# Seven half-size output products in place of eight, in sixteen chunks of a fused attention and feed-forward kernel

## The chip, the cores and the metric

One core of one Trainium2 chip. The metric is device time of the whole program in microseconds (us), lower is better. All times that are compared here are of runs in the fast state (the two probe runs are single executions of unknown state, and only their traces are used); a run's time is the median of its executions, and each ratio is against executions of the kernel before on the same chip. The experiments ran on several chips, where the kernel before took 569.3 to 569.8 us, and differences to the changed kernel go across them. Where I give a ratio it is the mean time of the fast runs of one kernel over that of the other's fast runs of the same rounds, so not quite the ratio of the medians that I quote. Profiles are single executions; their span is some 2 us shorter than the time.

## The reference

```python
# q, k, v: (4, 5824, 256) float32; w1, w2: 256x1024; w3: 1024x1024; w_out: 1024x256
qn = q / (norm(q, axis=1) + 1e-6);  kn = k / (norm(k, axis=1) + 1e-6)
a  = softmax(kn.transpose(0, 2, 1) @ qn / tau)     # one 256x256 matrix per batch
x  = (v @ a).reshape(23296, 256)
h  = ((x @ w1) * (x @ w2)) @ w3
out = h @ w_out                                     # (23296, 256) float32
```

## The kernel before

The kernel folds the softmax matrix into w1 and w2 (one pair `Wf` per batch) and w3 into w_out (one 1024x256 matrix `W_sb`). So each batch is out = ((v Wf1) * (v Wf2)) W. It works through a batch in 12 chunks: eleven of 512 tokens and a last one of 192. A chunk has 8 slots, one for each 128 of the 1024 features. In a slot TensorE makes a and b, ScalarE casts a to bf16 in SBUF, VectorE multiplies it with b (still in PSUM), and two slots later TensorE multiplies the product ab with its rows of W, four matmuls of 256 columns:

```python
def emit_ab(b, c, j):
    for w in range(2):                                   # a, then b
        t = psum.tile([P, 512], F32, tag="ab", ..., bufs=4)
        ...                                              # two matmuls of 512 columns
    a_sb = work.tile([P, 512], BF16, tag="a_sb", ..., bufs=4)
    nc.scalar.copy(a_sb[:, :n], tiles[0][:, :n])
    ...
        nc.vector.tensor_mul(ab, a_sb, tiles[1])
    pend.append((b, c, j, ab))

def emit_out(b, c, j, ab, only=None):
    lhs = [ab[:, i * P : (i + 1) * P] for i in range(4)]
    ...
        nc.tensor.matmul(tl[h][:, o, :], lhsT=lhsT, rhs=W_sb[:, j, :], ...)
    ...                                                  # after slot 7:
        nc.scalar.copy(o[:, 0:2, :], tl[0])
        nc.vector.tensor_copy(o[:, 2:4, :], tl[1])
```

While batch b runs, the scores and the softmax of batch b + 1 are made in between. A planner places them: it keeps a clock of TensorE's work, and each piece has a time at which it is put into the engines' queues. `t1` is when the scores end, 98 in the middle batches, which is in chunk 8. The softmax is this list (its second column is the time after `t1 + 1`):

```python
def norms():
    nc.vector.tensor_add(a1, accs[n][:, 0], accs[n][:, 1])
    nc.gpsimd.partition_all_reduce(tot, a1, P, ReduceOp.add)
...
    [(0.0, 0.0, norms), (0.0, 5.5, k_row)]
    + [(0.0, 5.5 + 1.2 * i, lambda i=i: k_step(i)) for i in range(4)]
    + [(0.0, 6.0, q_sums), (0.0, 8.5, lambda: q_norm(st["ss"]))]
    + [(0.0, 10.3 + 1.2 * ct, lambda ct=ct: scale(ct)) for ct in range(CT)]      # VectorE
    + [(0.0, 11.0 + 1.2 * ct, lambda ct=ct: exps(ct)) for ct in range(CT)]       # ScalarE
    + [(0.2, 14.6, sums)]                                                        # TensorE
    + [(0.43, 15.6 + 1.1 * i, lambda i=i: fold(i)) for i in range(8)]            # TensorE, then ACT or DVE
```

Of the kernel before, what the change touches and what calls it, by code (L numbers as in the profile page):

```python
# [12 lines left out]
F32 = DT.float32  # L13
BF16 = DT.bfloat16

P = 128
PIECE = 8
LAG = 2
LAG_END = 5
IN_BUFS = {"q": 5, "k": 6, "v": 3}  # L20
MM_COL = 1.0 / 2400.0
MM_FIX = 0.0025

# [2 lines left out]
def kernel(  # L26
# [73 lines left out]
    pieces = {}  # L100

    def new_piece(nm, n, pi):
        t = in_pool.tile([P, PIECE, C], BF16, tag=nm, name=f"{nm}_{n}_{pi}", bufs=IN_BUFS[nm])
        pieces[nm, n, pi] = t
        if pi == NP_ - 1:
            if nm != "v":
                nc.vector.memset(t[LEFT:, LAST, :], 0.0)
            nc.gpsimd.dma_start(out=t[:LEFT, LAST, :], in_=qk_main[nm, n][1])
# [332 lines left out]
    def at(t, cost, fn):  # L441
        seq[0] += 1
        agenda.append((t, seq[0], cost, fn))
# [12 lines left out]
        return vTt[:, ct, :]  # L456

    last_ab = [None]
    held = [None]

    def gate():

# [7 lines left out]
    def emit_ab(b, c, j):  # L470
        n = chunk_cols(c)
        tiles = []
        for w in range(2):
            t = psum.tile([P, 512], F32, tag="ab", name=f"{'ab'[w]}_{b}_{c}_{j}", bufs=4)
            for ct in range(CT):
                nc.tensor.matmul(  # L476
                    t[:, :n], lhsT=Wf[b][:, ct, w, j * P : (j + 1) * P], rhs=rhs_of(b, c, ct),
                    start=(ct == 0), stop=(ct == CT - 1),
                )
            tiles.append(t)  # L480
        a_sb = work.tile([P, 512], BF16, tag="a_sb", name=f"as_{b}_{c}_{j}", bufs=4)
        nc.scalar.copy(a_sb[:, :n], tiles[0][:, :n])  # L482
        if c == NCH - 1:
            if b % 2 == 0 and j == 0:
                lefts[b // 2] = work.tile([P, FT, 2, P + LEFT], BF16, tag="left", name=f"left_{b}", bufs=1)
            both = lefts[b // 2][:, j, b % 2, :]
            nc.vector.tensor_mul(both, a_sb[:, :n], tiles[1][:, :n])  # L487
            ab = both[:, :P] if b % 2 == 0 else both[:, LEFT:]
        else:
            if b == 0 and c < 2:  # L490

                if j % 4 == 0:
                    held[0] = in_pool.tile([P, 4, 512], BF16, tag="q", name=f"abq_{c}_{j}", bufs=IN_BUFS["q"])
                ab = held[0][:, j % 4, :]
            else:
                ab = work.tile([P, 512], BF16, tag="ab_sb", name=f"abs_{b}_{c}_{j}", bufs=8 * NDEF + 2)
            nc.vector.tensor_mul(ab, a_sb, tiles[1])  # L497
        pend.append((b, c, j, ab))
        last_ab[0] = ab
        clock[0] += 4 * (n * MM_COL + MM_FIX)  # L500

    def emit_out(b, c, j, ab, only=None):
# [42 lines left out]
            if only is None:  # L545
                del out_tiles[b, c]

    NDEF = 4

    def load_qk(n, pi):  # L550
        load_piece("q", n, pi)
        load_piece("k", n, pi)
# [17 lines left out]
    def transpose_w3():  # L570

        for h in range(FT // 2):
            m = in_pool.tile([P, 2, FT, P], BF16, tag="k", name=f"w3T_{h}", bufs=IN_BUFS["k"])
            nc.sync.dma_start_transpose(m, w3_bf[:, 2 * h : 2 * h + 2, :])
            w3T.append(m)

# [89 lines left out]
    def make_agenda(b):  # L666
        agenda.clear()
        clock[0] = 0.0
        n = b + 1
        if b == 0:  # L670
            at(0.5, 0.87, soft0[5])
            for i in range(4):
                at((1.7, 2.6, 3.5, 3.9)[i], 0.43, soft0[7 + i])
            at(0.0, 0.0, load_library)
            at(4.6, 0.5, lambda: transpose_half_on_pe(0, 0, 1, False))
            at(7.0, 0.5, lambda: transpose_half_on_pe(0, 1, 0, True))
            at(8.0, 0.5, lambda: transpose_half_on_pe(0, 1, 1, False))
            at(15.0, 0.0, transpose_w3)
            at(15.0, 0.0, lambda: transpose_piece(0, 2))
            for jt in range(FT):  # L680
                at(27.5 + 1.2 * jt, 0.87, lambda jt=jt: w_unit(jt))
            moves = [("qk", 1, 0, 29.0), ("v", 0, 3, 30.0), ("v", 0, 4, 30.5), ("qk", 1, 1, 44.0), ("qk", 1, 2, 45.0)]
            moves += [("qk", 1, 3, 53.0), ("qk", 1, 4, 55.0), ("v", 0, 5, 61.0), ("qk", 1, 5, 73.0)]
            moves += [("v", 1, 0, 88.0), ("v", 1, 1, 98.0), ("v", 1, 2, 120.0), ("qk", 2, 0, 130.0)]
            t0, t1 = 54.0, 113.0
        else:
            moves = [("v", b, 3, 1.0), ("qk", n, 1, 10.0), ("qk", n, 2, 17.0), ("v", b, 4, 26.0), ("qk", n, 3, 38.0)]
            moves += [("v", b, 5, 46.0), ("qk", n, 4, 58.0), ("qk", n, 5, 66.0)]
            moves += [("v", n, 0, 76.0), ("v", n, 1, 86.0), ("v", n, 2, 96.0), ("qk", n + 1, 0, 108.0)]
            moves = [m for m in moves if m[1] < B]  # L690
            t0, t1 = 16.0, 98.0

        before = (0, 2) if b == 0 else None
        for nm, m, pi, t in moves:
            if before is not None and not (nm == "v" and before == (m, pi - 1) == (0, 3)):
                at(t, 0.0, lambda w=before: hold(vTs[w[0]][1][:1, 0, :1] if w[1] == NP_ - 1 else vTs[w[0]][0][:1, w[1] * PIECE, 0, :1]))
            at(t, 0.0, gate)
            if nm == "qk":
                at(t, 0.0, lambda m=m, pi=pi: load_qk(m, pi))
                before = None  # L700
            else:
                at(t, 0.0, lambda m=m, pi=pi: load_piece("v", m, pi))
                at(t + 4.0, 0.0, lambda m=m, pi=pi: transpose_piece(m, pi))
                before = (m, pi)
        if n == B:
            agenda.sort()
            return
        units = score_units(n)
        for i, (cst, fn) in enumerate(units):
            at(t0 + (t1 - t0) * i / len(units), cst, fn)  # L710
        soft = soft_units(n)
        for cst, t, fn in soft:
            at(t1 + 1.0 + t, cst, fn)
        agenda.sort()

    for b in range(B):
        make_agenda(b)
        for c in range(NCH):
            for j in range(FT):
                run_due()  # L720
                emit_ab(b, c, j)
                npop = 0
                lag = LAG
                if b == B - 1 and c >= NCH - 2:
                    lag = LAG_END if c == NCH - 1 else LAG + (LAG_END - LAG) * (j + 1) // FT
                while w_ready[0] and len(pend) > lag and npop < 2:
                    emit_out(*pend.pop(0))
                    npop += 1
                    run_due()
        run_due(1e9)  # L730

    n = len(pend)
    for i, only in [(i, 1) for i in range(n - 1)] + [(i, 0) for i in range(n - 2)] + [(n - 1, 1), (n - 2, 0), (n - 1, 0)]:
        emit_out(*pend[i], only=only)


# [33 lines left out]
```

## Time and profile before

| | kernel before |
|---|---|
| time, median of 4 runs | 569.77 us (569.47 to 570.15) |
| span of the profile | 567.7 us |
| a slot of the last batch | 1.30 us, all of it TensorE |
| a chunk of the last batch | 10.40 us |
| start of chunk 8 to start of the next batch, second batch | 40.40 us |
| the same, third batch | 39.57 us |

All chunk times below are differences between the starts of the first a matmul of two chunks in the trace. The page and the timeline are read in the prediction.

### The profile page before, as it was taken

To read this page: it belongs to the slowest core of one execution; us is meant where nothing else is said; L and a number is where in the kernel's file an instruction comes from. 1 tells how busy PE (TensorE), PEld (TensorE's weight loads), DVE (VectorE), ACT (ScalarE), POOL (GpSimd) and SP (SyncE) were. 2 spreads that over 40 slices of the span, in tenths; PEclk is the share of its full clock that TensorE was granted. 3 is DMA by queue.
4 is the path that set the end of the run, shared out by engine and by line. 5 is a ranking of instruction groups with operands and counts; after the bars stand their busy time and mean duration, and the time that the engine had idled before them with its cause. 6 is when DMAs were issued, how large, how long until landed. Compare 5 with 4: busy or idle time off the path is not lost.

```text
span 567.7 us, 10095 instructions
## 1 busy us (share of the span) xinstructions
PE 557.6 (98%) x3755; PEld 355.4 (63%) x3755; DVE 375.4 (66%) x581; ACT 338.7 (60%) x627; POOL 77.9 (14%) x163
## 2 busy tenths in 40 slices
PE   8799999999999999999999999999999999999997
PEld 5664566776656666666656566666655655665655
DVE  1047645888966577888766668787876665565564
ACT  1057536777766577777675567777765554454453
POOL 4260013120111111121210101030120000000000
PEclk9999999999999999999999999999999999999999
DMA  9999989978455796595661595765740325221011
GB/s 213 211 182 209 173 171 237 226 164 192 115 142 121 143 192 148 90 193 123 145 149 75 97 219 117 155 120 121 185 112 39 85 74 149 64 68 71 38 70 61
DMA packets 75104, 77.45 MB, mean 136 GB/s; under 512 B 54192, under 2 KB 58800, under 8 KB 75056
## 3 DMA queue, kind: packets, MB, share of 16 engines
q0 software_dynamic: 15760, 38.93, 39.3%
q1 hardware_dynamic: 59008, 37.23, 22.0%
q10 hardware_dynamic: 288, 0.66, 0.4%
q8 instruction: 29, 0.48, 0.3%
q14 instruction: 19, 0.16, 0.1%
HBM read 78.91 MB, written 23.86 MB: 181 GB/s over the span
## 4 chain that ended last, share of the span: by engine, by line
PE 93%; DMA 5%; ACT 1%; POOL 0%; issue 0%; DVE 0%; ACTq 0%; POOLq 0%
PE o L521 28%; PE b L476 28%; PE a L476 28%; PE G L192 5%; DMA k<-in_k_dram 5%; PE fold L363 2%; PE w L649 1%; ACT kr L283 0%; PE quarter L389 0%; POOL k L111 0%; POOL q L111 0%; PE sqk L225 0%; PE row L271 0%; ACT e L322 0%; ACT Wf L398 0%
## 5 line engine op out<-in xcount | busy, mean ns | idle before, releaser
L497 DVE TENSOR_TENSOR abs<-as,b 128x512 bf16<-128x512 bf16 x336 | 230.6, 687 | 143.9 <-ACT as L482 131.4
L482 ACT CAST as<-a 128x512 bf16<-128x512 f32 (+1 forms) x384 | 215.9, 562 | 170.4 <-DVE abs L497 84.7
L476 PEld LDWEIGHTS <-Wf 128*128 128x128 bf16 x1536 | 149.0, 98 | 102.3 <-ACT Wf L398 0.6
L476 PE MATMUL a<-vT,Wf 128*128 128x512 bf16 x704 | 209.6, 379 | 0.4 <-ACT Wf L398 0.4
L476 PE MATMUL b<-vT,Wf 128*128 128x512 bf16 x704 | 209.6, 379 | 0.0
L521 PE MATMUL o<-W_sb,abs 128*128 128x256 bf16 x1344 | 201.5, 273 | 0.0
L521 PEld LDWEIGHTS <-abs 128*128 128x128 bf16 x1344 | 131.2, 98 | 79.8 <-issue 0.2
L201 DVE TENSOR_TENSOR acc<-acc,sq 128x1024 f32<-128x1024 f32 x66 | 80.4, 1219 | 0.6 <-ACT sq L189 0.6
L192 PE MATMUL G<-k,q 128*128 128x256 bf16 x276 | 49.8, 273 | 0.0
L189 ACT ACTIVATE sq<-q 128x512 f32<-128x512 bf16 x66 | 41.8, 633 | 0.0
L189 ACT ACTIVATE sq<-k 128x512 f32<-128x512 bf16 x66 | 41.5, 629 | 0.0
L464 POOL COPY gate_t<-abs 1x1 bf16<-1x1 bf16 x39 | 10.5, 269 | 171.7 <-DVE abs L497 168.8
L543 DVE COPY osb<-o 128x512 f32<-128x512 f32 x44 | 30.1, 685 | 0.9 <-PE o L521 0.9
L192 PEld LDWEIGHTS <-q 128*128 128x128 bf16 x276 | 27.0, 98 | 3.1
L542 ACT COPY osb<-o 128x512 f32<-128x512 f32 x44 | 25.8, 586 | 4.1 <-PE o L521 2.1
L468 POOL COPY gate_t<-vT 1x1 bf16<-1x1 bf16 x16 | 3.1, 193 | 158.8 <-DMA vT<-v 158.8
L111 POOL DMA_DIRECT2D q<-in_q_dram x28 | 15.1, 540 | 12.5 <-DMA k<-in_k_dram 5.5
L370 ACT ACTIVATE Wf<-fold,rs 128x512 bf16<-128x512 f32 x15 | 10.3, 687 | 10.9 <-PE fold L363 8.7
L283 ACT ACTIVATE kr<-row 128x256 f32<-128x256 f32 x1 | 0.4, 383 | 26.1 <-PE row L271 26.1
L363 PE MATMUL fold<-w,e 128*128 128x512 bf16 x56 | 15.0, 379 | 0.0
L487 DVE TENSOR_TENSOR left<-as,b 128x192 bf16<-128x192 bf16 x32 | 11.3, 354 | 5.1 <-ACT as L482 2.7
L497 DVE TENSOR_TENSOR abq<-as,b 128x512 bf16<-128x512 bf16 x16 | 10.8, 686 | 5.0 <-ACT as L482 4.5
(98 smaller groups left out, 242.3 us busy)
## 6 DMA issues: line engine op xcount, KB each, us to landing
out_dram<-osb SPq DMA_DIRECT2D x44, 512.0 KB, 3.3
k<-in_k_dram POOLq DMA_DIRECT2D x19, 512.0 KB, 8.3
v<-in_v_dram POOLq DMA_DIRECT2D x19, 512.0 KB, 5.2
q<-in_q_dram POOLq DMA_DIRECT2D x18, 512.0 KB, 5.8
w_wout<-in_moe_w_dram POOLq DMA_DIRECT2D x1, 2048.0 KB, 22.7
k<-in_k_dram POOLq DMA_DIRECT2D x4, 320.0 KB, 8.8
v<-in_v_dram POOLq DMA_DIRECT2D x4, 320.0 KB, 4.9
q<-in_q_dram POOLq DMA_DIRECT2D x3, 320.0 KB, 4.1
```

Source lines behind the costliest of these rows:

```text
L111: nc.gpsimd.dma_start(out=pieces[nm, n, pi][:, lo:hi, :], in_=qk_main[nm, n][0][:, pi * PIECE + lo : pi * PIECE + hi, :])
L189: nc.scalar.activation(out=dst[:, :, part, :], in_=src[:, o : o + 2, :], func=AF.Square)
L192: nc.tensor.matmul(G[:, ct, :], lhsT=qt[:, i, ct * P : (ct + 1) * P], rhs=kt[:, i, :], start=(pr == 0 and part == 0 and ct == 0), stop=(pr ...
L201: nc.vector.tensor_add(accs[n], accs[n], sqs[0])
L363: nc.tensor.matmul(m, lhsT=st["e"][:, c2, c1 * P : (c1 + 1) * P], rhs=w12[:, c2, w, lo:hi], start=(c2 == 0), stop=(c2 == CT - 1),)
L476: nc.tensor.matmul(t[:, :n], lhsT=Wf[b][:, ct, w, j * P : (j + 1) * P], rhs=rhs_of(b, c, ct), start=(ct == 0), stop=(ct == CT - 1),)
L482: nc.scalar.copy(a_sb[:, :n], tiles[0][:, :n])
L487: nc.vector.tensor_mul(both, a_sb[:, :n], tiles[1][:, :n])
L497: nc.vector.tensor_mul(ab, a_sb, tiles[1])
L521: nc.tensor.matmul(tl[h][:, o, :], lhsT=lhsT, rhs=W_sb[:, j, :], start=(j == 0 and o == 0), stop=(j == FT - 1 and (small or o == 1)), skip ...
L542: nc.scalar.copy(o[:, 0:2, :], tl[0])
L543: nc.vector.tensor_copy(o[:, 2:4, :], tl[1])
```

## The change

A chunk's output is a product of 512x1024 by 1024x256. Cut in halves along all three sizes, it is eight products of half-size blocks; Strassen's and Winograd's scheme does it with seven, at the price of sums of blocks. So 32 matmuls of 256 columns become 56 of 128 columns, seven eighths of the columns. The change does this in 16 of the 44 large chunks: ten of the last batch, and chunks 0, 8 and 9 of the second and third batch. A chunk of this kind stays open until all its slots are done; its seven products then stand in the first seven slots of the next chunk. VectorE makes four sums (128x1024, bf16, all operands in SBUF) and three joins (PSUM added to the output), ScalarE four keeps (PSUM copied to the output); one copy on each goes. The ab tiles must live longer, so q, k, v, ab and the rest share one ring of 22 buffers.

```diff
-IN_BUFS = {"q": 5, "k": 6, "v": 3}
+BIG_BUFS = 22
+    def seven(b, c):
+        return c < NCH - 2 if b == B - 1 else b > 0 and c in (0, NCH - 4, NCH - 3)
...
+        def sum1():
+            nc.vector.tensor_add(s1, a21, a22)
+        def p1():
+            st["o"] = work.tile([P, 4, D], F32, tag="o_sb", ...)
+            nc.vector.tensor_sub(s2, s1, a11)
+            product("A", a11, w1, True)          # 8 matmuls of 128 columns
+            keep(0, 0)
+        def p5():
+            nc.vector.tensor_sub(s3, a11, a21)
+            product("C", s1, t1, True)
+        def p6():
+            product("A", s2, t2)                 # adds to A
+            keep(0, 1)
+        def p7():
+            nc.vector.tensor_sub(s4, a12, s2)
+            product("A", s3, t3)
+            keep(1, 1)
+        def p2():
+            product("B", a12, w21, True)
+            join("B", 0, 0)
+        def p4():
+            join("C", 1, 1)
+            product("A", a22, t4)
+            keep(1, 0)
+        def p3():
+            product("C", s4, w22)                # adds to C
+            join("C", 0, 1)
...
+        if not seven(b, c):
+            pend.append((slot[0] + LAG, 1, lambda only=None: emit_out(b, c, j, ab, only)))
+        elif j == FT - 1:
+            fns = seven_products(b, c, *halves)
+            fns[0]()
+            pend.extend((slot[0] + 1, 2, fn) for fn in fns[1:])
```

(Cut: the four combined weight blocks, made once in the first batch, and the bookkeeping of the queue of pending work.)

More of the change, by code (lines that the diff above doesn't have):

```diff
@@ L102, in new_piece @@
     def new_piece(nm, n, pi):
-        t = in_pool.tile([P, PIECE, C], BF16, tag=nm, name=f"{nm}_{n}_{pi}", bufs=IN_BUFS[nm])
+        t = in_pool.tile([P, PIECE, C], BF16, tag="big", name=f"{nm}_{n}_{pi}", bufs=BIG_BUFS)
         pieces[nm, n, pi] = t
@@ L458, with combine_weights @@
     last_ab = [None]
-    held = [None]
+    halves = [None, None]
+    slot = [0]
+    comb = {}
+    def seven(b, c):
+        return c < NCH - 2 if b == B - 1 else b > 0 and c in (0, NCH - 4, NCH - 3)
+    def combine_weights(step):
+        b11, b12 = W_sb[:, 0:4, :P], W_sb[:, 0:4, P:]
+        b21, b22 = W_sb[:, 4:8, :P], W_sb[:, 4:8, P:]
+        if step == 0:
+            comb["T"] = in_pool.tile([P, 4, 4, P], BF16, tag="big", name="comb_T", bufs=BIG_BUFS)
+            for nm in ("S12", "S34"):
+                comb[nm] = in_pool.tile([P, 2, 4, 2 * P], BF16, tag="big", name=f"comb_{nm}", bufs=BIG_BUFS)
+            comb["f"] = in_pool.tile([P, 2, 4, P], F32, tag="big", name="comb_f", bufs=BIG_BUFS)
+        T, f = comb["T"], comb["f"]
+        if step == 0:
+            nc.vector.tensor_sub(f[:, 0], b12, b11)
+        elif step == 1:
+            nc.scalar.copy(T[:, 0], f[:, 0])
+            nc.vector.tensor_sub(f[:, 1], b22, f[:, 0])
+        elif step == 2:
+            nc.scalar.copy(T[:, 1], f[:, 1])
+            nc.vector.tensor_sub(T[:, 2], b22, b12)
+        else:
+            nc.vector.tensor_sub(T[:, 3], b21, f[:, 1])
@@ new lines, in seven_products, with product, quarter, keep @@
+    def seven_products(b, c, k1, k2):
+        T = comb["T"]
+        a11, a21 = k1[:, :, : 2 * P], k1[:, :, 2 * P :]
+        a12, a22 = k2[:, :, : 2 * P], k2[:, :, 2 * P :]
+        s1, s2 = comb["S12"][:, 0], comb["S12"][:, 1]
+        s3, s4 = comb["S34"][:, 0], comb["S34"][:, 1]
+        w1 = [W_sb[:, j, :P] for j in range(4)]
+        w21 = [W_sb[:, 4 + j, :P] for j in range(4)]
+        w22 = [W_sb[:, 4 + j, P:] for j in range(4)]
+        t1, t2, t3, t4 = ([T[:, i, j, :] for j in range(4)] for i in range(4))
+        st = {}
+        def product(nm, a, w, first=False):
+            if first:
+                st[nm] = psum.tile([P, 2, P], F32, tag="out", name=f"prod{nm}_{b}_{c}", bufs=3)
+            for j in range(4):
+                for i in range(2):
+                    nc.tensor.matmul(
+                        st[nm][:, i, :], lhsT=a[:, j, i * P : (i + 1) * P], rhs=w[j],
+                        start=(first and j == 0 and i == 0), stop=(j == 3), skip_group_check=True,
+                    )
+            clock[0] += 8 * (P * MM_COL + MM_FIX)
+        def quarter(r, d):
+            return st["o"][:, 2 * r : 2 * r + 2, d * P : (d + 1) * P]
+        def keep(r, d):
+            nc.scalar.copy(quarter(r, d), st["A"])
+        def join(nm, r, d):
+            nc.vector.tensor_add(quarter(r, d), st[nm], quarter(r, d))
+        def sum1():
+            nc.vector.tensor_add(s1, a21, a22)
+        def p1():
+            st["o"] = work.tile([P, 4, D], F32, tag="o_sb", name=f"osb_{b}_{c}", bufs=3)
+            nc.vector.tensor_sub(s2, s1, a11)
[21 more added lines that the diff above has]
+            join("C", 0, 1)
+            rows = out[b * N : b * N + NT * P, :].rearrange("(p i) c -> p i c", i=NT)
+            nc.sync.dma_start(out=rows[:, 4 * c : 4 * c + 4, :], in_=st["o"])
+        return [sum1, p1, p5, p6, p7, p2, p4, p3]
@@ L489, in emit_ab @@
         else:
-            if b == 0 and c < 2:
-                if j % 4 == 0:
-                    held[0] = in_pool.tile([P, 4, 512], BF16, tag="q", name=f"abq_{c}_{j}", bufs=IN_BUFS["q"])
-                ab = held[0][:, j % 4, :]
-            else:
-                ab = work.tile([P, 512], BF16, tag="ab_sb", name=f"abs_{b}_{c}_{j}", bufs=8 * NDEF + 2)
+            if j % 4 == 0:
+                halves[j // 4] = in_pool.tile([P, 4, 512], BF16, tag="big", name=f"abh_{b}_{c}_{j}", bufs=BIG_BUFS)
+            ab = halves[j // 4][:, j % 4, :]
             nc.vector.tensor_mul(ab, a_sb, tiles[1])
-        pend.append((b, c, j, ab))
         last_ab[0] = ab
+        slot[0] += 1
+        if not seven(b, c):
[4 more added lines that the diff above has]
+            pend.extend((slot[0] + 1, 2, fn) for fn in fns[1:])
         clock[0] += 4 * (n * MM_COL + MM_FIX)
@@ L546, in emit_out @@
                 del out_tiles[b, c]
-    NDEF = 4
     def load_qk(n, pi):
@@ L572, in transpose_w3 @@
         for h in range(FT // 2):
-            m = in_pool.tile([P, 2, FT, P], BF16, tag="k", name=f"w3T_{h}", bufs=IN_BUFS["k"])
+            m = in_pool.tile([P, 2, FT, P], BF16, tag="big", name=f"w3T_{h}", bufs=BIG_BUFS)
             nc.sync.dma_start_transpose(m, w3_bf[:, 2 * h : 2 * h + 2, :])
@@ L704, in make_agenda @@
                 before = (m, pi)
+        if b == 0:
+            for i in range(4):
+                at(115.0 + 3.0 * i, 0.0, lambda i=i: combine_weights(i))
         if n == B:
@@ L721 @@
                 emit_ab(b, c, j)
-                npop = 0
-                lag = LAG
+                lag = 0
                 if b == B - 1 and c >= NCH - 2:
                     lag = LAG_END if c == NCH - 1 else LAG + (LAG_END - LAG) * (j + 1) // FT
-                while w_ready[0] and len(pend) > lag and npop < 2:
-                    emit_out(*pend.pop(0))
-                    npop += 1
+                room = 2
+                while w_ready[0] and len(pend) > lag and pend[0][0] <= slot[0] and pend[0][1] <= room:
+                    _, size, fn = pend.pop(0)
+                    fn()
+                    room -= size
                     run_due()
@@ L733 @@
     for i, only in [(i, 1) for i in range(n - 1)] + [(i, 0) for i in range(n - 2)] + [(n - 1, 1), (n - 2, 0), (n - 1, 0)]:
-        emit_out(*pend[i], only=only)
+        pend[i][2](only=only)
 _INS = ['q', 'k', 'v', 'tau', 'moe_w1', 'moe_w2', 'moe_w3', 'moe_w_out']
```

## The prediction

> **What bounds the kernel now.** I read the page first, for the busy shares and the chain that ended last; then the timeline of the steady stretch of the last batch, for what sets a period; then the timeline of the first stage, where narrow matmuls already run; then the groups, for durations.
>
> ```profile
> span 567.7 us, 10095 instructions
> PE 557.6 (98%) x3755; PEld 355.4 (63%) x3755; DVE 375.4 (66%) x581; ACT 338.7 (60%) x627; POOL 77.9 (14%) x163
> PEclk9999999999999999999999999999999999999999
> PE 93%; DMA 5%; ACT 1%; POOL 0%; issue 0%; DVE 0%; ACTq 0%; POOLq 0%
> ```
>
> The chain of work that ended last is 93% TensorE; the 5% DMA is the first 30 us, which the change doesn't touch. Busy TensorE alone proves little, so look at starts:
>
> ```profile
> 504.76 0.59 PE L476 MATMUL a<-vT,Wf 128*128 128x512 bf16 x2
> 505.19 0.59 PE L476 MATMUL b<-vT,Wf 128*128 128x512 bf16 x2
> 505.39 0.59 ACT L482 CAST as<-a 128x512 bf16<-128x512 f32 x1 [0.71 <-DVE abs L497]
> 505.63 0.60 PE L521 MATMUL o<-W_sb,abs 128*128 128x256 bf16 x4
> 506.01 0.69 DVE L497 TENSOR_TENSOR abs<-as,b 128x512 bf16<-128x512 bf16 x1 [0.61 <-ACT as L482]
> 506.06 0.60 PE L476 MATMUL a<-vT,Wf 128*128 128x512 bf16 x2
> ...
> 508.61 0.69 DVE L497 TENSOR_TENSOR abs<-as,b 128x512 bf16<-128x512 bf16 x1 [0.61 <-PE o L521]
> 508.65 0.58 ACT L542 COPY osb<-o 128x512 f32<-128x512 f32 x1
> 508.66 0.59 PE L476 MATMUL a<-vT,Wf 128*128 128x512 bf16 x2
> 509.22 0.68 DVE L543 COPY osb<-o 128x512 f32<-128x512 f32 x1
> ```
>
> A slot (one of 8 feature blocks of a chunk of 512 tokens) takes 506.06 - 504.76 = 1.30 us: 0.43 for a, 0.43 for b, 0.435 for four output matmuls, with nothing between. Eight slots are 10.40 us. Four offsets matter below. ACT's cast starts 0.63 after the slot; DVE's product starts 1.25 after it, when the cast ends; two DVE instructions back to back start 0.61 apart though one lasts 0.69, so I count 0.08 less than the duration for each that queues. The fourth is the release, from an earlier stretch:
>
> ```profile
> 54.06 1.29 DVE L497 TENSOR_TENSOR abq<-as,b 128x512 bf16<-128x512 bf16 x2 [0.48 <-PE a L476]
> 54.24 0.59 PE L476 MATMUL a<-vT,Wf 128*128 128x512 bf16 x2
> 54.81 0.59 PE L476 MATMUL b<-vT,Wf 128*128 128x512 bf16 x2
> ```
>
> There b waited for DVE: the first product ended at 54.06 + 0.69 = 54.75, b started at 54.81, so 0.06 from an end to a released matmul.
>
> ```profile
> 9.94 1.04 PE L237 MATMUL G<-k,q 128*128 128x256 bf16 x8
> 10.82 1.06 PE L225 MATMUL sqk<-k 128*128 128x128 bf16 x16
> 11.71 0.59 PE L213 MATMUL warm_I-220_221<-warm 128*128 128x512 bf16 x2
> ```
>
> Sixteen 128-column matmuls, each with its own weights, took 11.71 - 10.82 = 0.89 us, 55.6 ns each. Eight of 256 columns took 0.88, 110 ns (108.5 to 109 in the steady stretch).
>
> ```profile
> L201 DVE TENSOR_TENSOR acc<-acc,sq 128x1024 f32<-128x1024 f32 x66 | 80.4, 1219 | 0.6 <-ACT sq L189 0.6
> L317 DVE TENSOR_TENSOR s<-G,kr 128x256 f32<-128x256 f32 x8 | 3.2, 416 | 0.2 <-ACT kr L283 0.2
> L538 ACT COPY osb<-o 128x256 f32<-128x256 f32 x4 | 1.5, 372 | 1.2 <-PE o L521 1.2
> ```
>
> These stand in for the added joins (0.416) and keeps (0.372), and give the full-rate cost of 1024 elements on DVE.
>
> **What the Trainium skill says.** "Perfetto Trace Analysis", Identifying the Most-Contended Engine: matmul busy time is a poor measure of distance from roofline. The trace agrees: the slot's starts show it, the 98% does not. "TensorE: Matmul & The Clock Gate", Back-to-back issue gap, puts a stream of weight load and 128-column matmul at about 81 ns each; with that, 56 would cost 4.5 us against 3.5 now and the change would lose a microsecond a chunk. The same page's warm isolated gap is 55.6 ns. Here the trace decides: 55.6 with a weight load per matmul. "VectorE: DVE Perf Modes", The perf-mode tier table: tensor_tensor on bf16 in SBUF runs two elements a cycle, fp32 or PSUM operands one. The trace agrees for the second half (1024 fp32 in 1.219 us); no instruction of this kernel shows the first. From that page's (N + 151)/0.96 with half of 1024 I estimate 0.69 us for an added bf16 sum, 0.61 queued.
>
> **The change part by part.** In 16 chunks 32 matmuls of 256 columns become 7 products of 8 matmuls of 128 columns. Saved: 32 x 109.2 = 3.494 us; spent: 56 x 55.6 = 3.114; net 0.380 a chunk, 6.1 us for 16. All of it lies on the bounding path, since TensorE never waits in these slots now.
>
> DVE per chunk: four sums of 1024 (0.61 each), three joins of 256 with a PSUM operand (about 0.34 queued), less one 0.61 copy. With eight products 8 x 0.61 + 2.44 + 1.02 = 8.3 us in a chunk of 10.0: under the bound. ACT: four keeps of 0.372 for one copy of 0.58, so 4.7 + 1.5 = 6.2. Neither becomes the bound on average, so single waits count. The build order shows the slots: seven with a, b and one product (0.863 + 0.445 = 1.308), one without.
>
> The wait that I think binds: the last product of a chunk accumulates on top of C, and must wait until DVE has joined C's earlier content to the output. In the build that join stands behind the a*b product of slot 5. It starts 1.25 + 0.61 = 1.86 after slot 5 begins, ends at 2.27, releases at 2.33. TensorE wants C at 1.308 + 0.863 = 2.17. So about 0.15 us of idle TensorE per chunk, wherever nothing else stands between: the ten chunks of the last batch and those made from chunks 0 and 8 of two batches, 14 in all: 2.1 us. Those made from chunk 9 have folds there and escape.
>
> The other waits pass, by the same offsets: the first sum must be ready 2.17 after slot 0 begins and ends at about 1.81; the keep of A between the second and third product on A ends 0.24 early; the buffer of b is needed 0.58 after DVE frees it at worst.
>
> Moved work: deferring a seven-product chunk leaves six slots with a and b alone (0.863 us). In chunk 8 of the two middle batches one fp32 accumulation (1.13 queued) falls among them. There b's buffer is normally free only 2 x 0.863 + 0.433 - 1.94 - 0.06 = 0.16 ahead, so DVE's delay of about 0.87 shows as about 0.7 of idle TensorE: 1.4 us for two. I add 0.2 for softmax pieces meeting the sums in chunk 10. Combining the weights (four DVE passes near 0.69, once) falls in slots of 1.30 us and is free. The common ring holds 22 buffers of 4 KB for 14 such and 34 of 1 KB; its loads wait for matmuls that, in the build order, were issued at least a chunk earlier, so I expect no new DMA wait.
>
> Sum: -6.1 + 2.1 + 1.4 + 0.2 = -2.4, so 567.1; I say 567.0.
>
> **The rivals.** First: no new wait; the join is quick enough or the accumulation falls well. Then 563.5, the pure column count. For it: slack is only missed by 0.15; a few tens of ns per instruction decide. Against: DVE's start at 1.25 is pinned by ACT's cast, which is pinned by TensorE. Second: the bf16 sums run one element a cycle, 1.22 us each (1.13 queued). Then DVE needs 8 x 0.61 + 4 x 1.13 + 1.02 = 10.4 us a chunk, more than TensorE's 10.0, and the first sum comes too late as well; 570 to 573. Against it: unit stride, two-byte types, all in SBUF. Third: narrow matmuls in between wide ones run nearer 81 ns; 16 x 1.04 us lost, about 586. The first stage speaks against it, where they stand between wide ones too. Fourth: the ring delays a load; one late score piece would show as microseconds in one place. The build order speaks against it.
>
> **Range and chances.** The saving on columns is certain to about 0.3 us. The waits could be 0 (563.5) or twice my sum (571). 8 in 10: 564.2 to 569.5. A gain over 2% would need 558, below what the columns allow: 0.01. Slower by 2% is the third rival: 0.02. Within 2%: 0.97.
>
> **What would show it.** 128-column products 0.445 us apart for eight: the column step. In the timeline of the last batch, a chunk period of about 10.17 us (10.02 without the wait, 10.40 before). A gap of 0.15 before the last product, released by DVE's join: the wait. Sums at 0.69 us, joins at 0.42, DVE near 8.3 us busy a chunk by the windows view. TensorE gaps near 0.7 in chunk 8 of the second and third batch, released by DVE's product. I'd be wrong if sums last 1.2 us, if DVE never idles in the last batch, or if TensorE idles on a DMA after the first 40 us.

## The result, and the profile after

The changed kernel takes 575.36 us (574.45 to 575.56, 4 runs) against 569.77: ratio 1.0096, 95% interval 1.0082 to 1.0111. It is 5.6 us slower, where I had said 2.8 us faster, and it is outside my range. The profiled spans differ by 5.0.

The page of the changed kernel (busy times, then the chain that ended last):

```profile
PE 556.6 (97%) x4130; PEld 356.2 (62%) x4139; DVE 423.3 (74%) x681; ACT 353.9 (62%) x677; POOL 82.3 (14%) x163
PE 90%; DVE 3%; DMA 3%; ACT 2%; issue 1%; POOL 0%; DVEq 0%; ACTq 0%; POOLq 0%
```

The chain went from 93% TensorE with no VectorE to 90% with 3% VectorE and 2% ScalarE. Both have small busy shares still; so the reader should look for places where TensorE waits for them, not for an engine that is full.

First the last batch, where nothing but slots and products runs. The timeline of the changed kernel at the end of a chunk's seven products (start, duration, engine, line, operation, output and inputs):

```profile
507.65 0.59 PE L574 MATMUL b<-vT,Wf 128*128 128x512 bf16 x2
507.76 0.42 DVE L518 TENSOR_TENSOR osb<-prodC,osb 128x256 f32<-128x256 f32 x1
508.24 0.61 PE L505 MATMUL prodC<-W_sb,comb_S 128*128 128x128 bf16 x8
508.68 0.59 PE L574 MATMUL a<-vT,Wf 128*128 128x512 bf16 x2
```

The product took 508.68 - 508.24 = 0.44 us for eight narrow matmuls. It could have started at 507.65 + 0.43 = 508.08; it started 0.16 later, 0.06 after VectorE's join of C ended. Both are the prediction's numbers, and so is the chunk: 10.18 us instead of 10.40. The groups of the changed kernel (busy us, mean ns):

```profile
L521 DVE TENSOR_TENSOR comb_S<-abh,abh 128x1024 bf16<-128x1024 bf16 x16 | 14.2, 887 | 0.5
L525 DVE TENSOR_TENSOR comb_S<-comb_S,abh 128x1024 bf16<-128x1024 bf16 x16 | 10.9, 683 | 0.0
```

The joins last 0.42 (above) and the second sums 0.683, as estimated. The first sums (L521) are the same operation on the same shape, and their mean is 0.887. A mean that is off by 0.2 over 16 is a few instances that are off by much. Two of them took 2.25 us, one in the second and one in the third batch. In those batches most of the time was lost, as the chunks show:

| stretch | before | after | after - before |
|---|---|---|---|
| batch 0, chunks 2 to 8 | 95.94 | 96.88 | +0.94 |
| batch 1, start of chunk 8 to start of batch 2 | 40.40 | 44.42 | +4.02 |
| batch 2, start of chunk 8 to start of batch 3 | 39.57 | 42.57 | +3.00 |
| batch 3, chunk 0 to the start of chunk 11 | 112.43 | 109.81 | -2.62 |

(Batch 0 has no seven-product chunk at all.) No wait on a DMA is new. Here is the timeline at the long first sum in batch 1; square brackets give the idle time before and what ended it:

```profile
282.59 3.23 POOL L262 PARTITION_ALL_REDUCE tot<-acc  x1 [2.43 <-DVE acc L260]
283.12 2.25 DVE L521 TENSOR_TENSOR comb_S<-abh,abh 128x1024 bf16<-128x1024 bf16 x1
285.43 0.62 PE L505 MATMUL prodC<-comb_T,comb_S 128*128 128x128 bf16 x8 [1.68 <-DVE comb_S L521]
```

The sum runs beside GpSimd's partition all-reduce and ends near its end, and TensorE waits for it. The slot is 3.16 us long instead of 1.31, and the same slot in batch 2 is 2.97: 1.85 + 1.66 = 3.5 us lost. In the kernel before, VectorE's product beside the same all-reduce takes its usual 0.69:

```profile
280.90 3.23 POOL L262 PARTITION_ALL_REDUCE tot<-acc  x1 [2.56 <-DVE acc L260]
281.68 0.69 DVE L497 TENSOR_TENSOR abs<-as,b 128x512 bf16<-128x512 bf16 x1 [0.28 <-ACT as L482]
```

And the timeline of the changed kernel one chunk later, at the products of chunk 9, where the softmax's scaling `s` (VectorE) and exponential `e` (ScalarE) come in:

```profile
294.59 0.69 DVE L521 TENSOR_TENSOR comb_S<-abh,abh 128x1024 bf16<-128x1024 bf16 x1
295.20 0.42 DVE L317 TENSOR_TENSOR s<-G,kr 128x256 f32<-128x256 f32 x1
295.65 0.51 ACT L322 ACTIVATE e<-s,r 128x256 bf16<-128x256 f32 x1 [1.85 <-DVE s L317]
296.07 0.56 ACT L580 CAST as<-a 128x512 bf16<-128x512 f32 x1
296.66 0.69 DVE L591 TENSOR_TENSOR abh<-as,b 128x512 bf16<-128x512 bf16 x1 [1.04 <-ACT as L580]
296.68 0.59 PE L574 MATMUL a<-vT,Wf 128*128 128x512 bf16 x2 [0.45 <-ACT as L580]
```

Read it from the top. The scaling stands in VectorE's queue behind a sum. ScalarE has the exponential at the head of its queue and sits idle for 1.85 us until the scaling is done. The cast of the next a stands behind the exponential, though its a was done by about 295.2. VectorE's next product waits 1.04 for that cast, and TensorE waits for the buffer that the cast frees. Every engine is idle for a while, none is full. The Trainium skill's page "PSUM — Partial Sum Buffer", Engine vs sequencer instructions, says that these engines' queues are strict FIFO; the lines above agree, the cast started only when the exponential had been fed.

So two theories came out of the trace. **A1**: VectorE's sum with two SBUF inputs and GpSimd's all-reduce exclude each other ("SBUF — State Buffer", Who interferes with whom, says that a VectorE instruction with two SBUF inputs contends with a GpSimd instruction that reads SBUF, and that the second to issue is blocked). The kernel before did not meet this: its product reads b from PSUM. **A2**: the order of the softmax's steps, the sums and the casts in two queues makes a convoy. Rivals: the ring of 22 buffers or the order of tiles costs the time; or VectorE and ScalarE simply have too much to do there.

### The profile page after: what moved, and what is told of

It is laid out like the page before. It is cut to its first block, busy times and chain, and to the rows that moved or that the text cites.

```text
span 572.7 us, 11027 instructions
## 1 busy us (share of the span) xinstructions
PE 556.6 (97%) x4130; PEld 356.2 (62%) x4139; DVE 423.3 (74%) x681; ACT 353.9 (62%) x677; POOL 82.3 (14%) x163
## 4 chain that ended last, share of the span: by engine, by line
PE 90%; DVE 3%; DMA 3%; ACT 2%; issue 1%; POOL 0%; DVEq 0%; ACTq 0%; POOLq 0%
PE a L574 26%; PE b L574 26%; PE o L621 18%; PE G L192 5%; PE prodA L505 5%; PE prodC L505 3%; DMA q<-in_q_dram 3%; PE fold L363 2%; PE prodB L505 1%; PE w L747 1%; PE G L237 1%; DVE abh L591 1%; DVE comb_S L521 1%; PE sqq L225 1%; ACT as L580 1%
## 5 line engine op out<-in xcount | busy, mean ns | idle before, releaser
L591 DVE TENSOR_TENSOR abh<-as,b 128x512 bf16<-128x512 bf16 x352 | 240.3, 685 | 98.7 <-ACT as L580 92.7
L574 PEld LDWEIGHTS <-Wf 128*128 128x128 bf16 x1536 | 144.9, 98 | 110.3 <-issue 4.8
L621 PE MATMUL o<-W_sb,abh 128*128 128x256 bf16 x896 | 131.0, 273 | 0.0
L621 PEld LDWEIGHTS <-abh 128*128 128x128 bf16 x896 | 87.4, 98 | 44.4 <-issue 0.2
L505 PEld LDWEIGHTS <-comb_S 128*128 128x128 bf16 x512 | 33.4, 98 | 22.6 <-DVE comb_S L521 4.8
L562 POOL COPY gate_t<-abh 1x1 bf16<-1x1 bf16 x39 | 13.1, 336 | 172.8 <-DVE abh L591 172.2
L515 ACT COPY osb<-prodA 128x256 f32<-128x256 f32 x64 | 23.8, 373 | 18.3 <-PE prodA L505 18.3
L505 PEld LDWEIGHTS <-abh 128*128 128x128 bf16 x384 | 25.5, 98 | 11.3
L643 DVE COPY osb<-o 128x512 f32<-128x512 f32 x28 | 19.2, 686 | 2.0 <-PE o L621 2.0
L505 PE MATMUL prodA<-comb_T,comb_S 128*128 128x128 bf16 x256 | 19.6, 219 | 0.5 <-DVE comb_S L530 0.5
L642 ACT COPY osb<-o 128x512 f32<-128x512 f32 x28 | 16.4, 585 | 4.3 <-PE o L621 3.5
```

Of the source, the lines that this page charges most:

```text
L505: nc.tensor.matmul(st[nm][:, i, :], lhsT=a[:, j, i * P : (i + 1) * P], rhs=w[j], start=(first and j == 0 and i == 0), stop=(j == 3), skip_ ...
L515: nc.scalar.copy(quarter(r, d), st["A"])
L562: nc.gpsimd.tensor_copy(gate_t, last_ab[0][:1, :1])
L574: nc.tensor.matmul(t[:, :n], lhsT=Wf[b][:, ct, w, j * P : (j + 1) * P], rhs=rhs_of(b, c, ct), start=(ct == 0), stop=(ct == CT - 1),)
```

## The experiments

All outputs are right. In the diffs "-" is the changed kernel unless said otherwise.

**Without chunks 8 and 9.**

```diff
-        ... else b > 0 and c in (0, NCH - 4, NCH - 3)
+        ... else b > 0 and c == 0
```

> The changed kernel with the seven products kept in the last batch and in chunk 0 of the two middle batches, and taken out of chunks 8 and 9 of the middle batches (12 chunks of 16 are left). Theory A (the loss sits where chunks 8 and 9 meet the softmax of the next batch: +4.0 and +3.0 us against the kernel before, from the start of chunk 8 to the start of the next batch's chunk 0): the time falls by 7.0 us from 575.4 to 568.4, about 1 us below the kernel before. Rival (the loss is the shared ring of buffers or the changed order of the tiles, which stays): the time falls by nothing, or rises by the lost saving of 4 x 0.2 us, to 575 to 576.

Measured: 568.42 us, ratio to the kernel before 0.9978 (0.9963 to 0.9993). The loss sits in these four chunks, to 0.1 us of the expected number; the ring, which is unchanged, doesn't cost it. Still, this says where, not why.

**The all-reduce on TensorE instead of GpSimd.**

```diff
-            nc.gpsimd.partition_all_reduce(tot, a1, P, ReduceOp.add)
+            if n == 1:
+                nc.gpsimd.partition_all_reduce(tot, a1, P, ReduceOp.add)
...
+        def reduce_on_pe():
...
+            nc.tensor.matmul(m, lhsT=ones_pp, rhs=st["a1"], start=True, stop=True)
+            nc.scalar.copy(st["tot"], m)
...
+            + [(1.07, 2.0, reduce_on_pe)] * (n > 1)
```

> All 16 chunks; the partition all-reduce of the second to last softmax goes from GpSimd to TensorE (a matmul of ones in fp32[...] and a copy on ScalarE). Theory A1 (VectorE's first sum of chunk 8, with both inputs in SBUF, is stopped while the all-reduce reads SBUF): that sum takes 0.69 us again instead of 2.25, TensorE's wait of 1.7 to 1.85 us for it goes in both batches, and the time falls by about 3.5 less two matmuls, to 573.3 to 574.2. Rival (the sum is slow for its data or for VectorE's backlog): it still takes 2.25 us and the time rises by about 2 us.

Measured: 571.26 us. All sixteen first sums (minimum, median, maximum ns) are alike now:

```profile
L527 DVE TENSOR_TENSOR comb_S<-abh,abh x16: 691/692/694, 189.3 to 548.2; 128x1024 bf16<-128x1024 bf16 x16
```

TensorE's waits for it are gone. But the gain, 4.1 us, is 2 to 3 more than I expected: chunk 10 also became shorter, 15.63 instead of 16.81 us. The 1.07 that I gave the planner for the matmul had shifted the softmax's steps against the slots. So I repeated it with the order held.

**The same, with the planner's clock left alone.**

```diff
-            + [(1.07, 2.0, reduce_on_pe)] * (n > 1)
+            + [(0.0, 2.0, reduce_on_pe)] * (n > 1)
```

> As the run with the all-reduce on TensorE, but with the cost of that work left out of the planner's clock, so that all other work keeps the order of the changed kernel. That run gained 4.1 us, 2.1 in chunk 9 to 10 and 1.85 in chunk 10 of the two middle batches (net of nothing), and its order in chunk 10 was another. Theory 1 (the collision alone is worth its two waits of 1.84 and 1.65 us; the rest was the other order): chunk 10 stays at 16.8 and 16.0 us and the time is 575.4 - 3.5 + 1.8 = 573.7. Theory 2 (the collision also makes the softmax late, and so costs in chunk 10 too): the time stays near 571.3.

Measured: 573.11 us, with chunk 10 at 16.81 and 15.97, the same as in the changed kernel. Theory 1: the collision is worth its two waits, and shifting the order by one matmul's time is worth some 1.9 us by itself. In the expectation's text "2.1 in chunk 9 to 10" was loosely put; the slots show 1.85 and 1.66 us of wait traded for 0.91 us of matmul in each batch.

**A probe of the collision in the kernel before.** The change is absent here; "-" is the kernel before.

```diff
             st["tot"] = tot
+            if n > 1:
+                probe("a", n)
+        def probe(nm, m):
...                                                      # d: a bf16 tile of 128x1024
+            if m == 2:
+                nc.vector.tensor_add(d, w12[:, 0, 0, :], w12[:, 1, 0, :])
+            else:
+                nc.vector.tensor_copy(d, w12[:, 0, 0, :])
...
+            + [(0.0, 4.2, lambda: probe("b", n))] * (n > 1)
```

(The rule that this expectation names is that of the page "SBUF — State Buffer", given above with A1.)

> The kernel before, with one useless VectorE instruction behind the partial sum that starts the partition all-reduce, and the same one again about 4 us later: in the third batch's softmax a sum of two SBUF tiles (128x1024, bf16), in the fourth's a copy of one SBUF tile of that size. Theory (GpSimd's all-reduce and a VectorE sum of two SBUF tiles exclude each other): the first sum takes about 2.2 to 3 us and ends when the all-reduce ends, the second takes 0.69; a*b products, which read PSUM, take 0.68 beside the all-reduce as before. By the Trainium skill's rule the copy is held too if it is in a mode that uses both ports; if only two inputs count, it takes the same time twice. Rival (sums of the middle batches are slow for another reason): both sums take 0.69.

The sum took 0.69, a miss, while the late copy in the fourth batch's softmax, which fell into the all-reduce's last part, took 0.93 instead of 0.42. The timeline says why (the last line is the late copy; its all-reduce ran from 413.46 to 416.79):

```profile
280.72 0.69 DVE L272 TENSOR_TENSOR probe_a<-w 128x1024 bf16<-128x1024 bf16 x1
280.90 3.60 POOL L262 PARTITION_ALL_REDUCE tot<-acc  x1 [2.47 <-DVE acc L260]
416.14 0.93 DVE L274 COPY probe_b<-w 128x1024 bf16<-128x1024 bf16 x1
```

The sum had started 0.18 us before the all-reduce, and now the all-reduce is the longer one, 3.60 instead of 3.23. So I put the probe one slot later ("-" is the first probe's run).

```diff
-                probe("a", n)      # directly behind norms
+            + [(0.0, 1.0, lambda: probe("a", n)), (0.0, 4.6, lambda: probe("b", n))] * (n > 1)
```

> The kernel before with the useless VectorE instruction one slot behind the start of the all-reduce (a sum of two SBUF tiles in the third batch's softmax, a copy of one SBUF tile in the fourth's), and the same about 4 us later. Theory (whoever starts second waits to the end): the all-reduce takes 3.23 us as without a probe; the first sum begins some 0.6 us into it and ends with it, so 2.2 to 2.6 us; the first copy likewise about 2 us, since the first probe's late copy took 0.93 and ended with the all-reduce; the later sum 0.69 and the later copy 0.42; the a*b products before and behind them 0.68 each. Rival (the sums of chunk 8 are slow for another reason): the first sum takes 0.69.

```profile
281.14 3.23 POOL L262 PARTITION_ALL_REDUCE tot<-acc  x1 [2.56 <-DVE acc L260]
281.56 2.37 DVE L270 TENSOR_TENSOR probe_a<-w 128x1024 bf16<-128x1024 bf16 x1
414.58 3.23 POOL L262 PARTITION_ALL_REDUCE tot<-acc  x1 [2.56 <-DVE acc L260]
414.99 2.10 DVE L272 COPY probe_a<-w 128x1024 bf16<-128x1024 bf16 x1
```

The sum takes 2.37 us and the copy with one input 2.10; four microseconds later they take 0.68 and 0.42. A1 holds in a kernel that has nothing else of the change, in both directions: who starts second is held. It costs time there too: chunk 9 becomes 0.87 and 0.61 us longer than in the kernel before. The traces agree with the skill's page, with one difference: sum and copy, less their own duration, both begin 2.1 us after the all-reduce's start (283.93 - 0.68 = 281.14 + 2.11; 417.09 - 0.42 = 414.58 + 2.09), not after its 3.23. That isn't the whole of it either: the first probe's late copy came 2.68 us after its all-reduce's start and was held until 3.19 (417.07 - 0.42 = 413.46 + 3.19). So the all-reduce blocks in at least two stretches, with a gap in which the second probe's copy ran; what it does in each no run shows.

**Exponentials, sums and folds later**, all else as in the changed kernel:

```diff
-            ... 11.0 + 1.2 * ct ... exps(ct)      14.6, sums      15.6 + 1.1 * i ... fold(i)
+            ... 12.3 + 1.2 * ct ... exps(ct)      15.4, sums      16.4 + 1.1 * i ... fold(i)
```

> All 16 chunks; the two exponentials of each softmax 1.3 us later in the planned order and the sums and folds after them 0.8 us later, so that the casts of the next slots stand before them on ScalarE. Theory A2 (in chunk 10 each exponential waits for a scaling that stands behind a sum on VectorE, and the cast of the next slot waits behind the exponential): the chunk 9 to 10 stretch of the middle batches loses 1.5 to 2 us less in each, and the time falls by 3 to 4 us to 571.5 to 572.5. Rival (VectorE or ScalarE has simply too much work there): within 0.7 us of 575.4.

Measured: 572.66 us, 2.7 less. The casts go ahead of the exponentials, ScalarE's idle time before the two in batch 1 falls from 1.85 and 1.42 to 0.32 and 0.55, and chunk 10 from 16.81 to 15.18. It falls short of the expected 3 to 4 because batch 2 gains little: its chunk 10 goes only from 15.97 to 15.65, with waits of 0.35 for a first sum and 0.46 for ScalarE's part of a fold left in it.

**The third join one product earlier.**

```diff
         def p2():
+            join("C", 1, 1)
             product("B", a12, w21, True)
             join("B", 0, 0)
         def p4():
-            join("C", 1, 1)
```

> All 16 chunks; the third join stands one product earlier, so that the last product finds its PSUM tile free. Theory (the wait of 0.15 us before the last product of each chunk of seven is the time that the join ends after the product before it, and no other wait takes its place): the wait goes from some 14 chunks, and the time falls by 2.1 us to 573.3. Rival (another wait ends at the same time, TensorE stops elsewhere): within 0.5 us of 575.4.

Measured: 573.21 us, 2.15 less; the slots of 1.46 are 1.31 in all 14 places. By the chunks of the two traces the gain is 1.8: chunk 10 of both middle batches became 0.15 longer, so there another wait took its place. The 0.15 in 14 places is settled.

**Chunk 8 alone, or chunk 9 alone, back to eight products.**

```diff
-        ... c in (0, NCH - 4, NCH - 3)
+        ... c in (0, NCH - 3)        # first run: chunk 8 back
+        ... c in (0, NCH - 4)        # second run: chunk 9 back
```

> Seven products in the last batch and in chunks 0 and 9 of the middle batches (chunk 8 back to eight products: 14 chunks). Theory (two independent losses: sum and all-reduce in chunk 8's products, and sums and exponentials in chunk 9's products): the all-reduce meets no sum, chunk 10 stays as slow: 575.4 - 3.5 (two waits) - 0.7 (stalls in chunk 8) + 0.8 = 572. Rival (chunk 10 is slow because the collision made the softmax late): nearly all of the loss goes and the time is 568 to 569.

> Seven products in the last batch and in chunks 0 and 8 of the middle batches (chunk 9 back to eight products: 14 chunks). Theory (two independent losses): the wait of 1.7 to 1.85 us for the first sum stays in both batches, chunk 10 is as before the change: 575.4 - 3.7 + 0.8 = 572.4. Rival (chunk 10 is slow because of the collision): the time stays at 574 to 576.

Measured: 569.20 without chunk 8, 572.31 without chunk 9. The second is as the theory of two losses expected. The first is 2.8 below it and close to the rival's 568 to 569, but that rival (a collision that makes the softmax late) is out, since chunk 10 stayed at 16.81 when the collision alone was removed. Here chunk 10 is 15.98 and 14.92 us, neither as slow as in the changed kernel (16.81, 15.97) nor quick. Yet chunk 9's sums are all still there. What changed is the order: the slots of chunk 8 cost the planner more again, and the first scaling now stands ahead of the first sum on VectorE. That points to places in queues, but doesn't show it, as chunk 8's products are gone too. It suggested a repair that drops nothing.

**The softmax 3.5 us earlier**, so that the all-reduce is over before the first sum of chunk 8 and the exponentials fall between the sums of chunk 8 and of chunk 9:

```diff
-            t0, t1 = 16.0, 98.0
+            t0, t1 = 16.0, 94.5
```

> All 16 chunks; in the two middle batches the scores and the softmax of the next batch end 3.5 us earlier in the planner's clock, so that the all-reduce is over before the first sum of chunk 8 and both scalings and exponentials fall between the sums of chunk 8 and those of chunk 9. Nothing else is changed. Theory (the loss is two meetings: all-reduce with sum, 3.5 us in both batches, and exponentials with sums, 4.4 us): the sum takes 0.69 us, TensorE's waits of 1.84 and 1.65 us are gone, chunk 10 falls from 16.8 and 16.0 us to about 14.2 in each; 575.4 - 7.9 = 567.5. Rival (VectorE and ScalarE have too much work in chunks 9 and 10, wherever it stands): the collision goes, 572, no more.

Measured: 570.85 us, 3.3 above the expectation. The first sums are all 0.69, so the collision is gone, and chunk 10 is 14.7 and 15.1. But a slot of 3.00 us has appeared at the end of chunk 9, in both batches. The timeline of this run:

```profile
289.00 0.41 DVE L317 TENSOR_TENSOR s<-G,kr 128x256 f32<-128x256 f32 x1
289.45 0.51 ACT L322 ACTIVATE e<-s,r 128x256 bf16<-128x256 f32 x1 [1.56 <-DVE s L317]
289.87 0.57 ACT L580 CAST as<-a 128x512 bf16<-128x512 f32 x1
290.46 0.69 DVE L591 TENSOR_TENSOR abh<-as,b 128x512 bf16<-128x512 bf16 x1 [1.05 <-ACT as L580]
291.07 0.42 DVE L518 TENSOR_TENSOR osb<-prodC,osb 128x256 f32<-128x256 f32 x1
291.54 0.61 PE L505 MATMUL prodC<-W_sb,comb_S 128*128 128x128 bf16 x8 [1.53 <-DVE osb L518]
```

It is the same convoy, and no sum stands in it: scaling, exponential, cast, product, and then the join, for which TensorE waits. The rival "too much work, wherever it stands" would fit this run as well; so the next one kept all the work and moved only what waits away from what it waits for.

**Earlier softmax, and a slot between its steps.**

```diff
-            t0, t1 = 16.0, 98.0
+            t0, t1 = 16.0, 94.5
-            ... 11.0 + 1.2 * ct ... exps(ct)      14.6, sums      15.6 + 1.1 * i ... fold(i)
+            ... 12.3 + 1.2 * ct ... exps(ct)      16.6, sums      18.8 + 1.1 * i ... fold(i)
```

> As the run with the earlier softmax (570.85), with the exponentials 1.3 us, the sums 2.0 and the folds 3.2 us later in the planner's clock than there, so that one slot or more lies between each step of the softmax and the next that waits for it on another engine. The work is the same. Theory Y (order in the queues): the slot of 3.0 us at the end of chunk 9 becomes 1.3 and chunk 10 stays at 14.5 to 15: 570.85 - 3.4 = 567.5. Theory X (too much work on VectorE and ScalarE there): within 0.7 of 570.85.

Measured: 568.06 us, ratio 0.9976 (0.9962 to 0.9989), 0.6 above the expectation. The slot of 3.00 is 1.86 and not 1.3, with a wait of 0.55 for the join still in it, and chunk 10 is 14.46 in both batches. With the same instructions as the changed kernel it is 7.3 us faster than that, and 2.8 faster than the run before it, which differs in the places of the exponentials, sums and folds alone. So the order in the queues is the cause of those 2.8; a load that is too large wherever it stands would have left them.

**Two PSUM tiles for a and two for b**, all else as in the changed kernel (the folds alternate between them):

```diff
-            t = psum.tile([P, 512], F32, tag="ab", ..., bufs=4)
+            t = psum.tile([P, 512], F32, tag=("pa", "pb")[w], ..., bufs=2)
```

> All 16 chunks; the four PSUM tiles of a and b become two of a and two of b, so that an a always waits for the cast of two slots before, not of one. Theory (the stalls of 0.40 us before an a or b in batch 0's chunk 2 and in chunk 8 come of the order in which the four tiles are handed out): the 0.8 us in batch 0 and the stalls of 0.4 and 0.33 in chunk 8 go: 575.4 - 1.5 = 573.9. Rival (they come of a late cast or product, whatever the tile): within 0.4 of 575.4.

Measured: 574.81 us, 0.55 less. The stretch in batch 0 goes from 96.88 to 96.07, so 0.8 us there did come of the order in which the four tiles are handed out; chunk 8 became 0.6 and 0.4 us longer. In its trace the two waits of an a in chunk 8 are gone, and b waits instead for VectorE's product, by starts 0.43 and 0.57 us in batch 1 and 0.76 in batch 2: that is the wait that the prediction had placed there. That a late b now has no other tile to use is my reading of it.

**Combinations.** Softmax earlier, join earlier and the two rings:

> All 16 chunks with the earlier softmax, the earlier third join and the two rings of PSUM tiles together. If the three causes are separate and nothing else is lost: 575.4 - 7.9 - 2.1 - 0.8 (the stalls of chunk 8 partly counted with the softmax) = 564.6, faster than both kernels and near the kernel before less the saved columns (563.5). Rival (causes overlap): 566 to 568.

Measured: 569.51 us, far from 564.6. It carries the convoy of the run with the earlier softmax. Next, only twelve chunks, with the earlier join and the two rings:

> Seven products in the last batch and chunk 0 of the middle batches (12 chunks), with the earlier join and the two rings: 568.4 - 1.6 (the join's wait in some 11 chunks) - 0.8 = 566.0. It shows what the change is worth without chunks 8 and 9; the kernel with all 16 and the earlier softmax should be 1.4 us below it.

Measured: 566.60 us (expected 566.0), ratio 0.9946. Last, all sixteen chunks with the two repairs of the softmax and the earlier join, without and with the two rings:

> The same with the third join one product earlier: 2.1 us less than that run, so 565.4 by theory Y and 568.8 by theory X.

> The same again with two PSUM tiles for a and two for b: the 0.8 us of stalls in batch 0 go, but the run with this edit alone gave back some 0.5 us in chunk 8; so 0 to 0.6 us below the run before it: 565.0 by theory Y.

Measured: 564.84 us without them (564.78 to 565.07, 5 runs; ratio to the kernel before 0.9919, 0.9906 to 0.9933), and 566.18 with them. The first is the best kernel: 4.6 us faster than before, 10.5 faster than the changed kernel. With the rings I had expected 0 to 0.6 less, and it is 1.3 more, a miss: by the traces the rings give back 0.3 and 0.4 us in chunk 8 and 0.5 in the first batch's end for the 0.8 that they save, which with smaller pieces makes 0.6; the rest of the 1.3 is not in these chunks and stays open. In the timeline of the best kernel at the place of the convoy TensorE no longer waits (289.76 + 0.43 = 290.19):

```profile
289.76 0.59 PE L574 MATMUL b<-vT,Wf 128*128 128x512 bf16 x2
290.13 0.51 ACT L322 ACTIVATE e<-s,r 128x256 bf16<-128x256 f32 x1 [0.23 <-DVE s L317]
290.19 0.61 PE L505 MATMUL prodC<-W_sb,comb_S 128*128 128x128 bf16 x8
290.54 0.56 ACT L580 CAST as<-a 128x512 bf16<-128x512 f32 x1
```

Its chunk 9 takes 10.03 us in both batches. VectorE is 74% busy in it, as in the changed kernel.

## Why the prediction was wrong, point by point

| term of the prediction's sum | predicted | measured | from |
|---|---|---|---|
| columns saved, 16 chunks | -6.1 | -5.9 | 10.40 - 10.18 + 0.15 = 0.37 a chunk |
| last product waits for the join | +2.1 | +2.1 | 14 slots of 1.46 instead of 1.31; join earlier: -2.15 (-1.8 by the traces) |
| b's buffer in chunk 8 | +1.4 | +0.7 | two late starts in the trace, 0.40 and 0.33, of an a and not of a b |
| softmax meets the sums | +0.2 | +4.0 | see below |
| first sum meets the all-reduce | not in it | +3.5 | slots of 3.16 and 2.97 instead of 1.31 |
| order of the PSUM tiles in batch 0 | not in it | +0.8 | two rings: 96.88 to 96.07 |
| sum | -2.4 | +5.2 | profiles +5.0, medians +5.6 |

The 4.0 is a remainder: with the all-reduce on TensorE and the order held, the two stretches from chunk 8 to the next batch are 43.49 and 41.83 us; less the 0.91 of the added matmul, the kernel before (40.40, 39.57) less two chunks' saving and plus one join's wait (-0.74 + 0.15), and the chunk 8 gaps, that leaves 2.36 and 1.61. Read directly, the late starts of TensorE's matmuls in chunk 10 (start less the start before it and that matmul's own time) add up to 2.3 and 1.4 us. The run with both repairs of the softmax gave 7.3 back, against 3.5 + 4.0.

**Right.** The column count and its step of 55.6 ns; the sums at 0.69 and joins at 0.42; the 0.15 us wait, its releaser and its number of places; no new DMA wait; batch 3 behaves to 0.01 us of the prediction's 10.17. The second and third rival (sums at one element a cycle, narrow matmuls at 81 ns) are out, and so is the fourth, a delayed load.

**Wrong.** The step that failed is the part of "The change part by part" that passes from the last batch to the middle ones. It says "The other waits pass, by the same offsets": offsets measured in the last batch, which has neither an all-reduce nor a softmax. There were two holes. For chunk 8 I placed "one fp32 accumulation" among the slots and didn't ask what GpSimd ran at that time; the all-reduce is in the trace of the kernel before, beside products with one input in PSUM, and the sums bring two SBUF inputs to that place. The 0.69 that I gave each sum holds for 14 of 16 first sums. And "I add 0.2 for softmax pieces meeting the sums in chunk 10" was sized as work added to a queue, when its cost is the wait of the next engine's queue: 4.0 us, twenty times the size. The average check (8.3 us of VectorE in a chunk of 10.0; the windows view gives 8.73 in 10.18) was near enough and told nothing of either.

**Half right.** There are stalls in chunk 8, together about half the size predicted, but the mechanism was another: an a waited, in batch 1 for ScalarE's cast of the slot before it (281.42, 0.40 late) and only in batch 2 for VectorE's product (416.84, 0.33 late). The same wait of an a for a cast, 0.40 twice, is the loss in batch 0, so that the size came half right by luck. That the four PSUM tiles are handed out in another order in the changed build, and cost 0.8 us in a batch that the change doesn't touch, I had not looked for. Why the order comes out differently is left open.

## What to carry to other kernels

Count a new instruction's cost in each stage where it will run, by what stands beside it in the other engines' queues; a busy share of 74% says nothing of a convoy. In strict queues leave a slot between an instruction and the one on another engine that waits for it (here that was worth 2.8 us), and keep VectorE's instructions with two SBUF inputs clear of GpSimd's all-reduce. When a change loses, first try to move its neighbours: here the same instructions in another order are 1.8% faster than the change as it was given.

## What the Trainium skill lacked or had wrong

- "SBUF — State Buffer", SBUF: two separate sides: the rule on two SBUF inputs and on who starts first is right, and so is its list that has a plain copy in it (0.42 us alone, 2.10 us beside the all-reduce). It says that the pair is held for the whole instruction. Here a sum or copy that came early in an all-reduce recorded with 3.23 us was held only until 2.1 us after its start, a copy that came at 2.68 us into another was held until 3.19, and between these a copy ran. Durations on GpSimd are rough in these profiles, so the ends of the stretches are estimates from VectorE's times.
- No page that I found gives what a partition all-reduce of 128x512 fp32 takes on GpSimd (3.23 us here, against 0.91 us of TensorE for a matmul of ones).
- "TensorE: Matmul & The Clock Gate", Back-to-back issue gap: its sustained gaps, about 81 ns for 128 columns and 131 for 512 with a weight load each, are not what these runs show: 56 ns and 216 ns, the isolated formula's values, in the midst of a/b slots.
- "PSUM — Partial Sum Buffer", Engine vs sequencer instructions: it states the strict queues, but no page that I found warns of the convoy that they make through two engines; here it cost 4.0 us with every engine under 75% busy but TensorE.
